# First attention layer: three query tiles of heads 0 to 15 first, projections and v tiles laid out over the steps

## The chip, the cores and the metric

One core of one Trainium2 chip runs the whole program. The metric is the device time of one execution in microseconds (us). Every run also has a span (first to last instruction, about 1.8 us less than its time) and a mean granted clock of the tensor engine (PE). Kernels are compared only within the same rounds. No run is over 1.5% above the fastest of its kernel, so all count as fast; only the state of e6, a single run, is unknown.

## The reference

Four layers in a row on x of shape 2048 x 576: attention A, gated MLP B, A, B, each with a LayerNorm ahead and a residual sum. The change touches only the first A.

```python
# A: 32 heads of 18 channels, each query sees 8 keys, 2 tokens apart
qkv = (x @ wqkv)                     # 576 -> 3*576
logits = einsum(q, k[window]) * Dh**-0.5 ; attn = softmax(logits)
o = einsum(attn, v[window]) ; return o @ wo
# B: z = gelu(x @ w_in); z1, z2 halves; z2 = layernorm(z2)
#    g = w_sp @ z2 + b_sp ; return (z1 * g) @ w_out
```

## The kernel before

Attention runs in 38 steps of manual order: a step is one tile of 112 queries and one half of the heads. Each step does logits (L_mm), the exponential on ScalarE (EXP) and the product with v (PV). All else of the layer is hung on the steps by a table: q and k projections (PG), v tiles (VW), output projection (WO), LayerNorm of the next layer (LN_...). The second half of the tokens is still being projected while the first steps run.

```python
# evacuation of a projection into staging, then moves into the row layout
if cb == 0 and d >= 3 and lent:
    stg_tiles[key] = lent[d - 3]              # first half, d=3,4: space of win2a
else:
    stg_tiles[key] = stgs[stg_rr[0] % NSTG]   # 3 staging buffers in turn
    stg_rr[0] += 1
...
for dst, src in moves:                        # up to 8 moves of 72 KB a group
    dma_rr[0] += 1
    self.dma(dst, src, eng=queues[dma_rr[0] % len(queues)])   # SP, GpSimd in turn
...
o_t = o_bufs[t % len(o_bufs)]                 # 3 buffers; VectorE writes o here
...
nc.sync.dma_start_transpose(out=oT[:, :, c0:c0 + nq], in_=o_t[:nq, :])
...
# projections of the second half: six ahead of step 0, one a step after it
pre, pgs = pgs[:6], pgs[6:]
for k_, (d, qk, cc) in enumerate(pgs):
    at(1 + k_ if li == 0 else (k_ * PG_END) // len(pgs), PG, d, qk, cc, True)
...
for s in range(NST):                          # natural order of the steps
    if s + 1 < NST:
        L_mm(s + 1)
        EXP(s + 1)
    PV(s)
    for f, a in table.pop(s, []):
        f(*a)
...
# next layer, B, tile 6 of its first pass: on GpSimd's queue
self.dma(bsp, self.B_b_sp.partition_broadcast(P), eng=nc.gpsimd)
```

bsp lies in the same buffer (ln_xn) as the last normalized tiles of layer A, so this load must wait until they have been transposed out; in the profile of before it waits 5.42 us for that.

The softmax here doesn't subtract the row's maximum and nothing guards it: scores larger than these inputs give would overflow.

## Time and profile before

| | before |
|---|---|
| time, median of 3 runs | 1190.21 us (1190.11 to 1192.29) |
| span of the profiled execution, granted clock | 1190.8 us, 0.998 |
| its time | 1192.6 us, one of its slower executions |

The lines that carry the argument stand in the prediction. First, the stretch from 60 to 70 us by the windows view: length, busy us of each engine, and as the last three figures the granted clock, the mean share of the 16 DMA engines and GB/s. Then all that VectorE waited for from 55 to 90 us (total, times, longest):

```profile
60.00:70.00 10.00, 10.00 (x177) 5.80 (x175) 6.97 (x16) 8.01 (x10) 4.50 (x8) 1.00 0.85 160
...
DVE stg L371 <- PE pp L402: 3.4, 9, 0.4
DVE rec L463 <- PE O_ps L457: 2.3, 7, 0.4
```

The reader is to see PE full, the DMA engines at 0.85, and a VectorE that waits only for PE, never for a transfer.

### The profile page before, as it was taken

How to read it: one execution, taken by the hardware profiler on the slowest of the kernel's cores; microseconds unless marked ns; L12 is line 12 of the kernel's file. 1: busy time of each engine (PE TensorE's matmuls, PEld its weight loads, DVE VectorE, ACT ScalarE, POOL GpSimd, SP SyncE). 2: the span in 40 equal slices, each digit the busy share in tenths (PEclk: the TensorE clock that was granted, in tenths of full speed). 3: DMA queues.
4: the chain of work that ended last, by engine and by line, in shares of the span. 5: the costliest groups of instructions: out<-in, count | busy, mean ns of one | idle time of the engine just before them, and what ended most of it. 6: DMA issues, size and time to landing. Idle time of an engine off the chain costs nothing.

```text
span 1190.8 us, 20761 instructions
## 1 busy us (share of the span) xinstructions
PE 1180.2 (99%) x8554; PEld 620.6 (52%) x8554; DVE 547.4 (46%) x1206; ACT 376.6 (32%) x593; POOL 281.5 (24%) x383
## 2 busy tenths in 40 slices
PE   8999999999999999999999999999999999999998
PEld 5567544444444444457755775444444444444677
DVE  8688587333233233245556786753233233233311
ACT  5578677210110110202156786760110110111000
POOL 4768685000000000001153877530000000000000
PEclk9999999999999999999999999999999999999999
DMA  8989992000000000049645999900000000000332
GB/s 195 200 163 199 181 224 65 23 4 9 12 12 12 12 1 11 12 139 291 169 98 117 203 227 196 202 14 9 12 12 1 12 12 12 12 1 28 125 105 73
DMA packets 178104, 101.21 MB, mean 85 GB/s; under 512 B 134336, under 2 KB 159360, under 8 KB 178009
## 3 DMA queue, kind: packets, MB, share of 16 engines
q1 hardware_dynamic: 165144, 78.13, 30.6%
q0 software_dynamic: 6512, 16.00, 5.4%
q10 hardware_dynamic: 6352, 5.75, 1.6%
q8 instruction: 67, 1.10, 0.4%
q14 instruction: 29, 0.23, 0.1%
HBM read 42.39 MB, written 16.53 MB: 49 GB/s over the span
## 4 chain that ended last, share of the span: by engine, by line
PE 94%; DMA 3%; POOL 1%; ACT 0%; issue 0%; SPq 0%; DVE 0%; ACTq 0%; DVEq 0%
PE pg L887 42%; PE pz L869 12%; PE po L941 12%; PE pz L791 11%; PE pp L402 5%; PE pw L494 3%; PE O_ps L457 3%; PE pv L379 3%; PE L_ps L437 2%; DMA oT<-o_t 2%; PE pzs L791 1%; DMA QK<-win2a 1%; POOL QK L77 1%; DMA wqk_sb<-in_A_wqkv_dram 1%; ACT P_sb L446 0%
## 5 line engine op out<-in xcount | busy, mean ns | idle before, releaser
L887 PE MATMUL pg<-Wq,Z 128*128 128x512 bf16 x2304 | 502.8, 379 | 0.0
L887 PEld LDWEIGHTS <-Z 128*128 128x128 bf16 x2304 | 225.3, 98 | 272.0
L891 DVE TENSOR_TENSOR g_tmp<-pg,ln_xn 128x512 f32<-128x512 f32 x144 | 99.6, 692 | 429.2 <-PE pg L887 429.2
L881 ACT ACTIVATE z1T<-pz 128x1024 bf16<-128x1024 f32 x72 | 73.7, 1024 | 513.8 <-PE pz L869 513.6
L77 POOL DMA_DIRECT2D wout<-in_B_w_out_dram x4 | 4.3, 1064 | 604.6 <-PE pg L887 604.6
L941 PE MATMUL po<-wout,Z 128*128 128x288 bf16 x1152 | 141.4, 286 | 0.0
L446 ACT ACTIVATE P_sb<-L_ps 128x896 bf16<-128x896 f32 (+1 forms) x152 | 126.7, 887 | 41.2 <-PE L_ps L437 40.6
L869 PE MATMUL pz<-xnT,w 128*128 128x512 bf16 (+1 forms) x640 | 136.0, 380 | 0.0
L941 PEld LDWEIGHTS <-Z 128*128 128x128 bf16 x1152 | 112.7, 98 | 28.8
L791 PEld LDWEIGHTS <-xnT 128*128 128x128 bf16 (+1 forms) x800 | 66.2, 97 | 81.0 <-issue 23.7
L791 PE MATMUL pz<-win2a,xnT 128*128 128x512 bf16 x384 | 104.8, 380 | 0.0
L892 DVE TENSOR_TENSOR Z<-g_tmp,z1T 128x512 bf16<-128x512 f32 x144 | 99.6, 692 | 9.7
L869 PEld LDWEIGHTS <-w 128*128 128x128 bf16 (+1 forms) x640 | 51.1, 97 | 80.0 <-issue 27.1
L402 PE MATMUL pp<-xnT,wqk_sb 128*128 128x512 bf16 x360 | 83.8, 382 | 0.5 <-DMA wqk_sb<-in_A_wqkv_dram 0.5
L805 ACT ACTIVATE zp<-pz 128x1024 bf16<-128x1024 f32 x64 | 65.5, 1024 | 36.6 <-PE pz L791 32.8
L951 DVE TENSOR_TENSOR x_new<-po,xo 128x288 f32<-128x288 f32 (+1 forms) x64 | 28.8, 455 | 87.6 <-PE po L941 83.5
L791 PE MATMUL pz<-win2b,xnT 128*128 128x512 bf16 (+1 forms) x256 | 65.7, 380 | 0.0
L807 DVE CUSTOM_DVE_ANT_0 Z<-zp 128x1536 bf16<-128x1536 bf16 x32 | 56.6, 1769 | 13.1 <-ACT zp L805 13.0
L77 POOL DMA_DIRECT2D QK<-stg x81 | 50.7, 631 | 36.3 <-DVE stg L371 21.0
L379 PE MATMUL pv<-wv_sb,xnT 128*128 128x288 bf16 (+1 forms) x380 | 55.8, 285 | 0.0
L242 POOL TENSOR_SCALAR ln_xn<-x_new,ln_mv,ln_rstd 128x576 bf16<-128x576 f32 x23 | 52.8, 2294 | 2.0
L402 PEld LDWEIGHTS <-wqk_sb 128*128 128x128 bf16 x360 | 33.2, 98 | 37.2 <-DMA wqk_sb<-in_A_wqkv_dram 1.0
(114 smaller groups left out, 916.9 us busy)
## 6 DMA issues: line engine op xcount, KB each, us to landing
xres<-x_new SPq DMA_DIRECT2D x48, 288.0 KB
xo<-xres SPq DMA_DIRECT2D x32, 288.0 KB
wout<-in_B_w_out_dram POOLq DMA_DIRECT2D x4, 1296.0 KB, 8.5
xo<-xres SPq DMA_DIRECT2D x8, 576.0 KB
w<-in_B_w_in_dram SPq DMA_DIRECT2D x16, 256.0 KB
QK<-stg POOLq DMA_DIRECT2D x53, 72.0 KB, 4.4
QK<-stg SPq DMA_DIRECT2D x41, 72.0 KB
xo<-in_A_x_dram SPq DMA_DIRECT2D x8, 288.0 KB
```

The source lines that it names most:

```text
L77: return eng.dma_start(out=out, in_=in_)
L379: nc.tensor.matmul(pv[:nk, 0:288], lhsT=self.xnT[:, c, QT * t:QT * t + nk], rhs=wv_sb[:, c, hh * 288:(hh + 1) * 288], start=(c == 0), stop ...
L402: nc.tensor.matmul(pp[:, :], lhsT=w, rhs=self.xnT[:, c, PADL + cc * 512:PADL + (cc + 1) * 512], start=(c == 0), stop=(c == 4))
L446: nc.scalar.activation(out=P_bufs[(2 * s + jp) % 4][:nk, :, :, 0:nq], in_=Lv[:nk, :, :, 0:nq], func=ACT.Exp, scale=scale)
L791: nc.tensor.matmul(pzvs[ci][:, sub * 512:sub * 512 + w], lhsT=self.xnT[r0:r1, c, PADL + i * P:PADL + (i + 1) * P], rhs=win2(c)[r0:r1, c0 + ...
L805: nc.scalar.activation(out=zp[:, c0:c0 + cn], in_=pzvs[ci][:, 0:cn], func=ACT.Gelu_apprx_tanh, accum_out=sums[:, ci:ci + 1])
L869: nc.tensor.matmul(pz1s[q // 2][:, q % 2, :], lhsT=w1[r0:r1, c, sub * P:(sub + 1) * P], rhs=self.xnT[r0:r1, c, PADL + q * 512:PADL + (q + ...
L881: nc.scalar.activation(out=z1T[:, q2 * 512:(q2 + 2) * 512], in_=pz1s[q2 // 2][:, :, :].rearrange("p a b -> p (a b)"), func=ACT.Gelu_apprx_ ...
L887: nc.tensor.matmul(pg[:, :], lhsT=Z[:, jj, i, sub * P:(sub + 1) * P], rhs=Wq[q][:, i, :], start=(i == 0), stop=(i == NS - 1))
L891: nc.vector.tensor_tensor(out=tmp[:], in0=pg[:, :], in1=bsp[:, qs], op=ALU.add)
L892: nc.vector.tensor_tensor(out=uT(jj)[:, sub, qs], in0=tmp[:], in1=z1Ts[jj, sub][:, qs], op=ALU.mult)
L941: nc.tensor.matmul(acc[hh], lhsT=uT(j // 2)[:, j % 2, i * P:(i + 1) * P], rhs=wouts[j // NJH][:, j % NJH, hh * 288:(hh + 1) * 288], start= ...
```

## The change

Its intent: let the first steps run on heads 0 to 15, whose rows are there early, and fill the steps that the exponential paces (1.85 us a step for 1.43 us of PE's work from 80.47 to 87.85 us of before) with projections, v tiles and output projections. Core of the diff:

```diff
+        seq = list(range(NST))
+        if li == 0:
+            seq[0:6] = 0, 2, 4, 1, 3, 5
...
-            self.load_wqk(nc.sync)
+            self.load_wqk(nc.sync, ("k", "q0", "q1", "k1"))
...
-            nvw0, nvw = 4, 9
+            nvw0, nvw = 4, 8
...
-        pre, pgs = pgs[:6], pgs[6:]
+        npre = 4 if li == 0 else 6
+        pre, pgs = pgs[:npre], pgs[npre:]
+        pg_at = ((0, 1, 3, 4, 5, 6, 6, 7, 7, 8, 8, 9, 10, 11, 12, 12) if li == 0 else ...)
...
-                if li == 0 and t == nvw:
-                    at(13 * hh, VW, t, hh, True)
...
+                    k_ = 2 if t == nvw else 12 + hh if t == nvw + 1 else 2 * t - 5 + hh
...
-            s = 2 * t + (6 if li == 0 and t < 10 else 5 if ...)
+            s = 10 + 2 * i if li == 0 and i < 8 else 2 * t + (5 if ...)
...
-                at(max(s + 4, 24 + (5 * i) // 4) if li == 0 else s + 4, LN_T, i)
+                at(s + 4 if li > 0 or i > 12 else 19 + 2 * i if i < 8 else 35 + (i - 8) // 2, LN_T, i)
         if li == 0:
+            for k_, part in ((2, (0, 0)), (3, (0, 1)), (5, (4, 0)), (6, (4, 1))):
+                at(k_, self.fill_window_rows, QK, 1, (part,))
...
+            at(0, lambda: nc.gpsimd.tensor_copy(out=rstds[:, 0:1], in_=self.xnT[:, 0, ...]))
+            w2l = self.load_win2a(nc.gpsimd)
```

The small GpSimd copy near the end reads the last transposed input, so that the six win2a weight loads behind it on GpSimd start only when that input has landed.

More of the change, by code (lines that the diff above doesn't have):

```diff
@@ L185, in make_ident, with fill_window_rows @@
                                 base=0, pattern=[[-1, P]], channel_multiplier=1)
-    def fill_window_rows(self, QK, half):
+    def fill_window_rows(self, QK, half, parts=((0, 0), (0, 1), (4, 0), (4, 1))):
         nc, n = self.nc, self.cfg.S // 2
@@ L193, in fill_window_rows @@
         c0 = PADL + half * n
-        for g0 in (0, 4):
-            for a in range(2):
-                nc.vector.tensor_copy(out=QK[:, a, g0:g0 + 4, c0:c0 + n].rearrange("p g (k x) -> p g k x", x=256),
-                                      in_=self.pat[:, a, None, None, PADL:PADL + 256].to_broadcast([P, 4, n // 256, 256]))
+        for g0, a in parts:
+            nc.vector.tensor_copy(out=QK[:, a, g0:g0 + 4, c0:c0 + n].rearrange("p g (k x) -> p g k x", x=256),
+                                  in_=self.pat[:, a, None, None, PADL:PADL + 256].to_broadcast([P, 4, n // 256, 256]))
     def H_tile(self, name):
@@ L284, in zero_right, with load_wqk @@
         nc.vector.memset(R["wo"][64:128, 4, :], 0.0)
-    def load_wqk(self, eng):
+    def load_wqk(self, eng, names=("k", "q", "k1")):
         R = self.right
-        for c0, n, w0 in ((D, 512, D + 64), (0, D, 0), (D + 512, 64, D)):
+        parts = dict(k=(D, 512, D + 64), q=(0, D, 0), q0=(0, 256, 0), q1=(256, D - 256, 256), k1=(D + 512, 64, D))
+        for c0, n, w0 in (parts[k_] for k_ in names):
             self.dma(R["wqk"][:, :, w0:w0 + n], self.A_wqkv[0:512, c0:c0 + n].rearrange("(c p) n -> p c n", p=P), eng=eng)
@@ L425, in layer_A @@
         NST = 2 * NT
+        seq = list(range(NST))
+        if li == 0:
+            seq[0:6] = 0, 2, 4, 1, 3, 5
+        pbi = {s: 2 * k_ for k_, s in enumerate(seq)}
         L_tiles = {}
@@ L445, in EXP @@
                 Lv = L_ps[:, :, 0:4 * QT].rearrange("p a (b c) -> p a b c", c=QT)
-                nc.scalar.activation(out=P_bufs[(2 * s + jp) % 4][:nk, :, :, 0:nq], in_=Lv[:nk, :, :, 0:nq], func=ACT.Exp,
+                nc.scalar.activation(out=P_bufs[(pbi[s] + jp) % 4][:nk, :, :, 0:nq], in_=Lv[:nk, :, :, 0:nq], func=ACT.Exp,
                                      scale=scale)
@@ L457, in PV @@
                         nc.tensor.matmul(O_ps[:, idx * (DH + 1):(idx + 1) * (DH + 1)],
-                                         lhsT=P_bufs[(2 * s + jp) % 4][:nk, jj, ftl, :],
+                                         lhsT=P_bufs[(pbi[s] + jp) % 4][:nk, jj, ftl, :],
                                          rhs=v_ext[:nk, t, 16 * hf + idx, :], start=True, stop=True)
@@ L509, in LN_XN @@
                 k_, m = divmod(i - 4, 3)
-                xn = stgs[(2 + k_) % NSTG][:].rearrange("p a b -> p (a b)")[:, 640 * m:640 * (m + 1)]
+                xn = stgs[(1 + k_) % NSTG][:].rearrange("p a b -> p (a b)")[:, 640 * m:640 * (m + 1)]
             tails[i]["xn"] = self.ln_xn(tails[i]["x"], P, mv, rstd, nmr, eng="pool", xn=xn)
@@ L648, in layer_A @@
             nvw0, nvw = 0, 4
-        for t in range(nvw0, nvw - (1 if li == 0 else 0)):
+        for t in range(nvw0, nvw):
             for hh in range(2):
-                VW(t, hh, li == 0)
+                VW(t, hh, li == 0 and t > 5)
         pieces = []
@@ L667, in layer_A @@
         PG_END = 14
-        pre, pgs = pgs[:6], pgs[6:]
+        npre = 4 if li == 0 else 6
+        pre, pgs = pgs[:npre], pgs[npre:]
+        pg_at = ((0, 1, 3, 4, 5, 6, 6, 7, 7, 8, 8, 9, 10, 11, 12, 12) if li == 0
+                 else [(k_ * PG_END) // len(pgs) for k_ in range(len(pgs))])
         for k_, (d, qk, cc) in enumerate(pgs):
-            at(1 + k_ if li == 0 else (k_ * PG_END) // len(pgs), PG, d, qk, cc, True)
+            at(pg_at[k_], PG, d, qk, cc, True)
         for t in range(nvw, NT):
             for hh in range(2):
-                if li == 0 and t == nvw:
-                    at(13 * hh, VW, t, hh, True)
-                else:
-                    at(2 * t - 2 + hh, VW, t, hh, 2 * t - 2 + hh >= PG_END and hh == 0)
+                if li == 0:
+                    k_ = 2 if t == nvw else 12 + hh if t == nvw + 1 else 2 * t - 5 + hh
+                else:
+                    k_ = 2 * t - 2 + hh
+                at(k_, VW, t, hh, k_ >= PG_END and hh == 0)
         for i in range(NS):
             t = -(-(i + 1) * P // QT) - 1
-            s = 2 * t + (6 if li == 0 and t < 10 else 5 if t < NT - 5 else 4 if t < NT - 3 else 3)
+            s = 10 + 2 * i if li == 0 and i < 8 else 2 * t + (5 if t < NT - 5 else 4 if t < NT - 3 else 3)
             at(s - 5, XO, i)
@@ L686, in layer_A @@
             if i < NS - 1:
-                at(max(s + 4, 24 + (5 * i) // 4) if li == 0 else s + 4, LN_T, i)
+                at(s + 4 if li > 0 or i > 12 else 19 + 2 * i if i < 8 else 35 + (i - 8) // 2, LN_T, i)
         if li == 0:
+            for k_, part in ((2, (0, 0)), (3, (0, 1)), (5, (4, 0)), (6, (4, 1))):
+                at(k_, self.fill_window_rows, QK, 1, (part,))
             at(0, self.load_wo, nc.sync)
-            for f in reversed(self.load_win2a(nc.gpsimd)):
-                at(0, f)
+            at(0, lambda: nc.gpsimd.tensor_copy(out=rstds[:, 0:1], in_=self.xnT[:, 0, PADL + S - 1:PADL + S]))
+            w2l = self.load_win2a(nc.gpsimd)
+            for k_ in (3, 5, 4, 2, 1, 0):
+                at(0, w2l[k_])
         at(PG_END + 2, alloc_win2b)
@@ L698, in layer_A @@
             if k_ == (2 if li == 0 else 0):
-                L_mm(0)
-                EXP(0)
-            PG(d, qk, cc, li > 0 or k_ < 4, q2)
-            if li == 0 and k_ == 3:
-                self.fill_window_rows(QK, 1)
-        if li == 0:
-            VW(nvw - 1, 0, False)
-            VW(nvw - 1, 1, False)
+                L_mm(seq[0])
+                EXP(seq[0])
+            PG(d, qk, cc, True, q2)
         for s in range(NST):
             if s + 1 < NST:
-                L_mm(s + 1)
-                EXP(s + 1)
-            PV(s)
+                L_mm(seq[s + 1])
+                EXP(seq[s + 1])
+            PV(seq[s])
             for f, a in table.pop(s, []):
```

## The prediction

> **What bounds the kernel now.** I read the page's engine table first, then the granted clock by slice, then the matmul engine's timeline of the first attention layer, because the diff acts only where the layer index is 0 (the other attention layer gets the same lists as before).
>
> ```profile
> PE 1180.2 (99%) x8554; PEld 620.6 (52%) x8554; DVE 547.4 (46%) x1206; ACT 376.6 (32%) x593; POOL 281.5 (24%) x383
> ...
> L446 ACT ACTIVATE P_sb<-L_ps 128x896 bf16<-128x896 f32 (+1 forms) x152 | 126.7, 887 | 41.2 <-PE L_ps L437 40.6
> ```
>
> PE has work in 1180 of 1190.8 us: it is the bound, and the change gives it the same matmuls in another order (the built programs have the same number of PE instructions). So the change can win only what PE loses to waits, to stretched groups and to a slow clock. 1190.8 - 1180.2 = 10.6 us is idle in the whole program. The exponential (L446) takes 0.92 us for a full tile here, and each attention step needs two of them.
>
> The places of loss, in order of time:
>
> ```profile
> 14.47 7.73 PE L402 MATMUL pp<-xnT,wqk_sb 128*128 128x512 bf16 x35 [0.55 <-DMA wqk_sb<-in_A_wqkv_dram]
> ...
> 47.28 0.89 PE L437 MATMUL L_ps<-QK 32*128 32x112 bf16 x15
> 48.86 0.22 PE L437 MATMUL L_ps<-QK 32*128 32x112 bf16 x1 [0.69 <-DMA QK<-win2a]
> ...
> 50.90 2.29 PE L402 MATMUL pp<-xnT,wqk_sb 128*128 128x512 bf16 x5
> ...
> 82.71 0.37 PE L437 MATMUL L_ps<-QK 32*128 32x112 bf16 x8 [0.27 <-ACT P_sb L446]
> ...
> 98.69 0.37 PE L437 MATMUL L_ps<-QK 32*128 32x112 bf16 x8 [0.32 <-ACT P_sb L446]
> ...
> 125.22 0.79 PE L494 MATMUL pw<-wo_sb,oT 128*128 128x288 bf16 x5 [0.59 <-DMA oT<-o_t]
> ...
> 131.51 1.39 PE L494 MATMUL pw<-wo_sb,oT 128*128 128x288 bf16 x10 [1.23 <-DMA oT<-o_t]
> ```
>
> Columns: start, duration, what, and in brackets the idle time before it. The reader is to see a wait for the q weights; the second logits group (heads 16 to 31 of tile 0) held by its q/k rows, 16 matmuls taking from 47.28 to 49.01 where a free group takes 0.33; a projection of 2.29 us where its neighbours take 1.24; small waits for the exponential; and waits for the transposed output at the end. The windows by the microsecond explain the 2.29:
>
> ```profile
> 48.00:49.00 1.00, 0.32 (x5) 0.14 (x2) 1.00 (x2) 0.90 (x1) 1.00 (x2) 1.00 1.30 223
> ...
> 51.00:52.00 1.00, 1.00 (x5) 0.31 (x3) 0.71 (x2) 1.00 (x2) 0.05 (x1) 0.50 1.06 395
> 52.00:53.00 1.00, 1.00 (x3) 0.15 (x1) 0.00 (x0) 0.33 (x1) 0.00 (x0) 0.50 1.09 286
> ```
>
> The first figure after the length is PE, the third from the end the granted clock: half, some 2 us after PE was only a third busy. No other five-microsecond window of the program has a clock below 1.
>
> [...]the four windows from 50 to 54 have 0.76, 0.50, 0.50 and 0.54, which makes 0.5 + 1 + 1 + 0.9 = 3.4 us at half.[...]at 99.99 VectorE had waited 1.59 us for an output transpose[...]
>
> **The change part by part.** Clean costs from the chain of waits: logits group 0.33, PV group 0.49, one q/k projection 1.09, one v half tile 0.62, one output half tile 0.61.
>
> (a) q weights in two pieces. The first load shrinks from 576 to 256 columns: the 0.55 us wait should mostly go. I count 0.3, as it pulls the whole start forward only if nothing else is late.
>
> (b) Order 0, 2, 4, 1, 3, 5. The late rows belong to heads 16 to 31. Before, 6 projections, one logits group and 2 v halves stood between the v stretch and that logits group; after, 6 projections, 3 logits groups and 2 PV groups. That is 2x0.33 + 2x0.49 - 2x0.62 = +0.4 us of cover, and the last of those rows no longer share the DMA engines with the six 288 KB weight loads, which began at 45.99 and now wait for the last transposed input. The loss was 49.01 - 47.28 - 0.33 = 1.4; I expect 0.9 to 1.0 left. Gain 0.4.
>
> (c) The clock. The slow stretch cost 2.29 - 1.24 = 1.05 on the projection and about 0.25 on the groups around it, 1.3. [...]I give an even chance that it goes: gain 0.65.
>
> (d) Even spreading. From 53.13 to 65.73 six steps took 12.60, 2.10 each, where PE's work is 1.09 + 0.33 + 0.49 = 1.91: the loop logits, two exponentials (2 x 0.92 plus hand-over), logits sets the step. Loss 0.19 x 7 = 1.3. From 80.47 to 87.85 four steps without projection or v took 7.38, 1.85 each against 0.33 + 0.49 + 0.61 = 1.43: loss 1.6. From 96.45 to 102.59 three steps, two without output projection, took 6.14 against 4.93: loss 1.2, part of it the late output transpose. In all 4.1. After, I count by the table of steps: steps 0, 1, 3, 4, 5, 9 with one projection lose 0.19 each (1.1), step 14, which has no v half, 0.4, steps 33 and 34, whose v halves went earlier, 0.8; the output projections of tiles 0 to 7 now fill steps 10 to 25 without a gap. Left 2.3, gain 1.8.
>
> (e) VectorE: the pattern fill of the second half, 4 copies of 1.22 us, moves from one block into steps 2, 3, 5, 6. The fullest, step 6, has 0.72 (reciprocal and scaling) + 2 x 0.69 + 1.22 = 3.3 us for 3.0 of PE: up to some 1 us of lag, which the four single banks should absorb. No gain, a risk.
>
> (f) End of the layer: waits of 0.59 and 1.23 for output transposes stay; there is less v work beside them now. I count 0.
>
> Sum: 0.3 + 0.4 + 0.65 + 1.8 = 3.15 us. 1190.2 - 3.15 = 1187.1.
>
> **The rivals.** First: the wait only moves. If the rows of heads 16 to 31 land no earlier than 48.8 (their last issue, at 44.65, waited for an earlier transfer, and the chain of waits goes back over the queue to the evictions of about 26 us), the early start earns nothing, the clock still drops, and at the end the moved v halves lengthen the wait for transposes. Then some 1 us remains: 1189. For it: the page's chain shows these transfers as the setter. Against: there are three more groups of PE work before it. Second: VectorE or the staging buffers become the wait. Projections now come in pairs at steps 6 to 8, and the staging buffer of step 7 was sent off only at step 4; a queue-and-land time of 4.4 us (page, transfers of 72 KB) against about 7 us of steps is close once Pool's six weight loads of 0.85 us each stand ahead. [...]1 to 3 us come back: 1190 to 1191. Third: the whole loss goes, the clock stays up, no wait for the rows: 1.4 + 1.3 + 3 + 0.5 gives 6 us, 1184.
>
> **Range and chances.** The prediction is 1187.1 us; the range 1184.0 to 1190.2 spans the best and nearly the worst rival. A change of 2% is 24 us; everything that PE loses in this layer is about 11, so faster by over 2% has a chance of 0.01, slower (a hang-up of the queues I don't see) 0.01, within 2% 0.98.
>
> **What would show it.** Right: no or shorter wait at the fourth logits group (tile 0, heads 16 to 31), no half clock near 50 us, no exponential waits between 80 and 101, and the first matmul of the next layer, now at 129.67, some 3 us earlier, with everything after it unchanged in length. Wrong: a bracket with a transfer of staging rows before a VectorE eviction, PE waits for evictions in steps 6 to 8, waits for output transposes above 2 us at the end, or a second slow-clock stretch. The number fails most easily in (c), all or nothing, and in (d), where the loop may pace steps that I take as full.

The length of the half-clock stretch: by windows of 0.25 us the clock is 1.00 up to 50.50, 0.50 to 0.53 from there to 53.75 and 0.64 in the window after. VectorE's wait of 1.59 us ahead of 99.99: that PE was late by it was not shown. The even chance in (c) is the author's estimate, and the trace shows for it only that half clock began some 2 us after a microsecond with PE at 0.32. The sum came to 0.3 + 0.4 + 0.65 + 1.8 = 3.15 us, and so to 1187.1 us.

Three more readings have their figures here. In (b), the weight loads were issued from 45.99 us on, the last row move landed at 48.8 us, and the DMA share from 48 to 49 us was 1.30; that parting them would help was an estimate. In (d), that the exponentials set the step rests on the step times quoted there and on PE's three waits for them from 53 to 103 us, 0.9 us in all. In (e), the four single banks are four tiles of the kernel (`bufs=4`), and that they absorb the lag was an estimate.

## The result, and the profile after

| | before | changed |
|---|---|---|
| median in the first rounds | 1190.28 us (1190.11 to 1192.29, 4 runs) | 1192.87 us (1191.88 to 1194.37, 4 runs) |
| span, clock of the profiled execution | 1190.8 us, 0.998 | 1190.2 us, 0.999 |
| ratio of fast runs, 95% interval | | 1.0019 (1.0002 to 1.0036) |

Ratios are the mean time of one kernel's fast runs over that of the other's fast runs of the same rounds, so not quite the ratio of the medians quoted. Within 2% the two are the same, as predicted; but the time is 5.8 us above the predicted 1187.1 and outside the range. That the two profiled spans are nearly equal is chance: the execution profiled of before was one of its slow ones.

PE's timeline of the changed kernel (start, duration, group, in brackets the idle time ahead of it), at the places that answer to those shown of before:

```profile
12.94 8.80 PE L402 MATMUL pp<-xnT,wqk_sb 128*128 128x512 bf16 x40
...
47.41 0.65 PE L441 MATMUL L_ps<-QK 32*128 32x112 bf16 x16
...
73.60 0.77 PE L498 MATMUL pw<-wo_sb,oT 128*128 128x288 bf16 x5 [1.56 <-DVE stg L371]
80.98 0.37 PE L441 MATMUL L_ps<-QK 32*128 32x112 bf16 x8 [0.43 <-ACT P_sb L450]
...
151.65 0.81 PE L798 MATMUL pz<-win2a,xnT 128*128 128x512 bf16 x3 [1.59 <-ACT zp L812]
```

The wait for the q weights is gone: 40 projection matmuls in one piece. The fourth logits group (tile 0, heads 16 to 31), at 47.41, has no wait. From 80 to 101 us one wait for the exponential is left, 0.43 us, where before there were three of 0.85 us together. But two stops are new, 1.56 us behind VectorE's eviction into staging and 1.59 us in the next layer, behind the activation of a z tile (the zp stop). The same views as before, from 60 to 70 us and of VectorE's waits from 55 to 90 us, and three steps of the chain of waits ahead of the stop at 73.60:

```profile
60.00:70.00 10.00, 9.69 (x131) 5.04 (x129) 6.66 (x14) 6.46 (x8) 6.14 (x10) 1.00 1.20 169
...
DVE stg L371 <- DMA QK<-stg: 6.1, 2, 3.5
DVE x_new L501 <- PE pw L498: 2.5, 2, 2.0
...
63.88 0.79 SPq L77
...
64.72 8.02 DMA QK<-stg
...
72.86 0.70 DVE stg L371
```

VectorE now waits 6.1 us for moves out of the staging buffers; one of them, issued by the SP queue, took 8.02 us to land; and the DMA engines' share is 1.20: over 1, so the times of the packets under way add up to more than one per engine. The last figure of the line, what was moved, hardly rose, from 160 to 169 GB/s: the packets took longer, they did not carry much more.

The stop at 151.65 has its cause on GpSimd. Its lines in the changed kernel:

```profile
146.25 0.64 POOL L77 DMA_DIRECT2D ln_xn<-in_B_b_sp_dram x1 [6.60 <-DMA xnT<-ln_xn]
146.92 0.59 POOL L829 TENSOR_TENSOR z_rstd<-z_rstd,neg_half 128x1 f32<-128x1 f32 x1
```

The bias-row load waits 6.60 us for the last transposes of the LayerNorm output, and the small z_rstd operation, on which the normalization and in the end PE depend, stands behind it. In the kernel before that load started at 147.00 with 5.42 us of waiting, 11.7 us after PE's last output projection (done at 135.31); in the changed kernel it started 13.7 us after it (132.58). PE came 2.7 us earlier and the load only 0.75 us; so the load lagged 2.0 us more behind PE, and what had been hidden was now a stop. The load's line before:

```profile
147.00 0.64 POOL L77 DMA_DIRECT2D ln_xn<-in_B_b_sp_dram  x1 [5.42 <-DMA xnT<-ln_xn]
```

A table from PE's timelines, worked out: for each stretch the distances from start to start of PE's groups, less their clean cost (the clean costs of the prediction). The last row is the time from the end of the last output projection to the first matmul of the spatial product (pg), less its shortest value of 77.09. The columns are the profiled executions of before (two), of the changed kernel (three), and of the changed kernel with the projections as before (two, explained below). A recount from the traces gives the same cells within 0.5 us. Each of three columns holds a stretch of 3.4 us at half clock, which stretches PE's groups (ten output matmuls took 2.16 us in e1, 1.39 before): before near 51 us, e1 from 129 to 133 us, e2 from 74 to 78 us.

| PE time lost, us | before | before, e1 | changed | changed, e2 | changed, e13 | e11 | e14 |
|---|---|---|---|---|---|---|---|
| 40 to 55 | 2.8 | 1.7 | 1.2 | 1.6 | 1.7 | 2.9 | 2.0 |
| 55 to 78 | 1.1 | 1.1 | 2.8 | 3.9 | 4.2 | 1.4 | 2.2 |
| 78 to 103 | 3.4 | 3.1 | 2.2 | 1.7 | 2.9 | 1.9 | 1.7 |
| 103 to 138 | 2.8 | 3.4 | 1.3 | 1.7 | 2.0 | 2.3 | 1.8 |
| hand-over to the next layer | 0.0 | 0.0 | 1.8 | 1.6 | 1.2 | 1.1 | 0.5 |

The spreading did what it was meant to do after 78 us, and it was paid for twice: from 55 to 78 us and at the hand-over.

### The profile page after: what moved, and what is told of

Read it like the earlier page. It is cut to its first block, busy times and chain, and to the rows that moved or that the text cites. A ratio compares the mean times of both kernels' runs of the same rounds, so it can differ in the third digit from the quotient of the medians.

```text
span 1190.2 us, 20761 instructions
## 1 busy us (share of the span) xinstructions
PE 1177.7 (99%) x8554; PEld 619.9 (52%) x8554; DVE 546.0 (46%) x1202; ACT 377.2 (32%) x597; POOL 282.3 (24%) x384
## 4 chain that ended last, share of the span: by engine, by line
PE 94%; DMA 2%; DVE 2%; POOL 1%; issue 1%; ACT 0%; SPq 0%; POOLq 0%; DVEq 0%
PE pg L894 42%; PE pz L876 12%; PE po L948 12%; PE pz L798 10%; PE pp L402 5%; PE pv L379 4%; PE pw L498 3%; PE O_ps L461 2%; PE L_ps L441 2%; PE pzs L798 1%; DMA QK<-stg 1%; DMA oT<-o_t 1%; DMA xnT<-ln_xn 0%; POOL stg L241 0%; ACT P_sb L450 0%
## 5 line engine op out<-in xcount | busy, mean ns | idle before, releaser
L899 DVE TENSOR_TENSOR Z<-g_tmp,z1T 128x512 bf16<-128x512 f32 x144 | 99.7, 692 | 10.1 <-DVE g_tmp L898 0.5
L876 PEld LDWEIGHTS <-w 128*128 128x128 bf16 (+1 forms) x640 | 51.1, 97 | 80.0 <-issue 27.1
```

The source lines that it names most:

```text
L876: nc.tensor.matmul(pz1s[q // 2][:, q % 2, :], lhsT=w1[r0:r1, c, sub * P:(sub + 1) * P], rhs=self.xnT[r0:r1, c, PADL + q * 512:PADL + (q + ...
L899: nc.vector.tensor_tensor(out=uT(jj)[:, sub, qs], in0=tmp[:], in1=z1Ts[jj, sub][:, qs], op=ALU.mult)
```

## The experiments

Eighteen runs were made, on four chips; six of them repeat a kernel (e1 the one before, e2 and e13 the changed one, e6, e14 and e17 earlier variants); runs that stand in one group shared their rounds. "V waits" are the waits of VectorE from 55 to 90 us for transfers.

### First group: are the result and its waits repeatable, and does the tail count?

**e1_before_again**: the kernel before, unaltered.

> The unchanged kernel once more, for a second profile and ten more times. The profile on record had one stretch of half clock (3.4 us, about 1.3 us lost) and its run took 1192.6 us where the other runs took 1190.1 to 1190.4. Theory C (chance events): the usual run has no half-clock stretch or no long wait for q/k rows, so part of the predicted gain was never in the median; then this profile, if its run takes about 1190.2, has a clock of 1.00 near 50 us and a span near 1188.5. Rival: the half clock is there in the fast runs too (span near 1190.8 or clock 0.5 near 51 us with a run near 1190.2), and the loss of the changed kernel lies elsewhere.

1192.16 us (1191.26 to 1194.92), ratio 1.0004. Half clock at 50 us, a term of the prediction, is not in its profile (nor in those of e4 and e8): it was an accident of the execution that had been profiled. The profile of e1 has such a stretch elsewhere, from 129 to 133 us. The wait for the q weights, the prediction's term (a), is not in these three profiles either.

**e2_after_again**: the changed kernel, unaltered.

> The changed kernel once more, for a second profile and to see whether its runs again fall into two groups near 1191.9 and 1194. Theory A (tail): PE stops about 1.6 us some 20 us into the next layer, waiting for the activation of a z tile whose buffer Pool has not released, in this profile too. Theory B (staging): a wait of VectorE for q/k rows to leave a staging buffer stops PE 1 to 3 us near 71 us in this profile too. If one of the two is missing here while the time is the same, it is not the cause of the loss.

1193.04 us (1191.38 to 1193.70), ratio 1.0005 (0.9987 to 1.0023). Two theories stood at this point: A, the gain is lost at the hand-over to the next layer (the zp stop); B, it is lost to the staging buffers, reused too early. The profile has both: a stop of 1.72 us at 74.10 on the eviction into staging, V waits of 5.3 us for staging and 1.2 us for oT, the DMA share from 60 to 70 us at 1.17, and a zp stop of 1.44 us.

**e3_after_bsp_sp** and **e4_before_bsp_sp**: in the changed kernel and in the one before,

```diff
-                self.dma(bsp, self.B_b_sp.partition_broadcast(P), eng=nc.gpsimd)
+                self.dma(bsp, self.B_b_sp.partition_broadcast(P), eng=nc.sync if li == 1 else nc.gpsimd)
```

> The changed kernel with one line of the next layer altered: the load of the bias row, which stands at the head of Pool's queue there and waits for the last input transposes, goes to the SP queue (first mixer layer only). Theory A: Pool releases the z tiles in time, the stop of 1.6 us goes, and the time falls by 1.0 to 1.8 us against e2. Theory B: the stop near 71 us is the whole loss and this changes the time by less than 0.4 us.

> The same line altered in the kernel before, where the profile shows no stop of PE in the next layer although Pool waits 5.4 us for the same load. Theory A: the time stays within 0.4 us of e1, since nothing there waited. If it falls by more than 1 us, the load held up the kernel before as well, and the gain of e3 says nothing of the change.

e3: 1193.26 us (1190.78 to 1197.47), ratio 1.0016; e4: 1192.69 us (1190.21 to 1196.08), ratio 1.0011. In e3 the stop on zp is gone and the hand-over is back at 77.10 us, so the cause of that stop is shown. (In this execution PE came late, at 139.3 us, which alone could hide it; e17, with the same edit and PE at 133.2 us, has 77.09 us as well.) The time did not follow: the executions spread over 6.7 us, and the one profiled had a stop of 3.68 us on staging and two stretches at half clock (mean clock 0.994). In e4 there was nothing to gain. So the tail alone does not explain the result.

### Second group: is it the staging buffers?

**e5_after_lent** and **e6_after_lent_bsp** (its label is a slip: it ran the same kernel as e5, as its expectation says): the changed kernel, with the second halves of d=3 and d=4 staged in two input buffers that are free by then.

```diff
                 if cb == 0 and d >= 3 and lent:
                     stg_tiles[key] = lent[d - 3]
+                elif cb == 1 and d >= 3 and lent:
+                    stg_tiles[key] = spent[d - 3][:]...   # spent = [x1, x3]
```

> The changed kernel with one thing taken away: the second-half q and k projections of channel groups d=3 and d=4 are staged in two spent input buffers (free since the first LayerNorm), so they no longer wait until the moves of the first half have left the staging buffers. Theory B (the compressed projections reuse staging too early): the stop of the projections on VectorE between 60 and 80 us (1.56, 1.72 and 3.68 us in the three looks at the changed kernel) is under 0.3 us, VectorE waits under 0.5 us on the moves QK<-stg there, the last projection of the first layer ends by 70 us, and the span is 1.5 us or more under the 1190.2 to 1191.3 us of the changed kernel if no chance stretch at half clock falls in. Theory A (the gain is lost only at the hand-over to the next layer): the last PV of the first layer comes 1 to 2 us earlier, but the stop on zp (1.4 to 1.6 us) grows to 2 to 3 us and the span stays within 1 us of the changed kernel.

> Second look at the same kernel as the run before it, for the waits alone: the stop on staging is again under 0.3 us if theory B holds, and the zp stop again at 1.4 us or more if theory A holds as well.

e5: 1192.89 us (1190.64 to 1196.13), ratio 1.0011 (0.9995 to 1.0027); e6, one run, 1194.60 us. The staging wait is gone and the time is not better. VectorE's waits for transfers in e5, and where PE stopped:

```profile
DVE o_t L470 <- DMA oT<-o_t: 5.0, 2, 3.3
DVE x_new L503 <- DMA xo<-in_A_x_dram: 3.6, 1, 3.6
...
61.80 0.58 PE L404 MATMUL pp<-xnT,wqk_sb 128*128 128x512 bf16 x1 [1.84 <-DVE o_t L470]
...
86.79 0.55 PE L463 MATMUL O_ps<-v_ext,P_sb 128*128 128x19 bf16 x16 [1.80 <-DVE x_new L503]
```

Two other transfers took its place, the transpose of the attention output and the load of the residual: VectorE waited 5.0 and 3.6 us for them, and PE 1.84 and 1.80 us for VectorE. Theory B, staging alone, falls. The profile of e6 differs: PE waited 1.53 us for rows at 49.42, half clock followed, and then the DMA share from 60 to 70 us was only 0.96 and VectorE's waits for transfers 2.4 us.

**e7_after_lent_bsp**: e5 with the edit of e3. **e8_before_lent**: the kernel before with the edit of e5.

> Both suspected causes taken away: spent input buffers as staging, and the bias row of the second layer loaded by the SP queue, so that GpSimd's queue is not held up by it. If both theories hold, neither the stop on staging nor the stop on zp is in the profile, the distance between the last PV and the first PE group of the second layer is back to about 77 us (before: 77.1; changed: 78.9), the span is 1187 to 1188.5 us and the time 1188 to 1190 us, 0.15 to 0.4% under the kernel before. If the time is still that of the kernel before although both stops are gone, a third cause is at work.

> Control: the kernel before with the same spent buffers. VectorE waited there only 0.8 us for staging and the tensor engine not at all, so both theories expect the same time within 0.15% (1190 to 1192 us on this chip) and the same waits.

e7: 1192.96 us (1189.48 to 1195.91), ratio 1.0014; the hand-over is at 77.09 us, but V waits are 4.1 us for oT and 2.9 us for xo, with a stop of PE of 2.24 us at 84.40. A third cause was at work, as its expectation put it. e8: 1191.03 us, ratio 0.9997: no change, as the control should have it.

### Third group: what makes the transfers land late?

Theories by now: the SP queue is full of issues (C1), the DMA engines are full (C2), the tile order shortens the reuse of the three o buffers from 5 to 3 steps (D), or the compressed projections are the root of it all.

**e9_lent_moves_1to2**: e5 with the moves of the second half 1 to 2 on SP and GpSimd.

```diff
-            at(pg_at[k_], PG, d, qk, cc, True)
+            at(pg_at[k_], PG, d, qk, cc, True, q2 if li == 0 else (nc.sync, nc.gpsimd))
```

> Changed kernel with spent buffers as staging (as e5), and the moves of the second token half shared 1 to 2 between the SP and the GpSimd queue in place of 1 to 1. In e5 and e6, where staging was free, VectorE waited 3.34 us for oT<-o_t and 3.60 us for an xo load in place of staging. Theory C1 (the SP queue, which issues the moves one after the other at about 0.8 us each, with the oT transposes and xo loads among them, is full from 51 to 84 us): with a third fewer moves on SP it has gaps again, the oT and xo waits of VectorE between 55 and 90 us fall from 5 to 9 us to under 2 us, no stop of the tensor engine over 0.5 us there, last PV of the first layer by 127.5 us, span about 1188.5 us. Theory C2 (the DMA engines themselves are full): the same bytes move, so the waits stay at 3 us or more, on whatever lands last. Theory D (the tile order shortens the reuse of the three o buffers): the 3.3 us wait for oT<-o_t near 61 us stays, the xo wait may go.

1195.15 us (1193.93 to 1196.55), ratio 1.0029. VectorE's waits for oT and xo fell to 1.5 and 1.0 us (5.0 and 3.6 in e5), so the SP queue had its part. But the moves now land late from the other queue, and PE waits for the rows itself:

```profile
91.05 0.62 PE L443 MATMUL L_ps<-QK 32*128 32x112 bf16 x2 [2.29 <-DMA QK<-x_in]
```

**e10_lent_w2late**: e5 with the win2a loads at steps 17 to 27.

```diff
-            for k_ in (3, 5, 4, 2, 1, 0):
-                at(0, w2l[k_])
+            for n_, k_ in enumerate((3, 5, 4, 2, 1, 0)):
+                at(17 + 2 * n_, w2l[k_])
```

> Changed kernel with spent buffers as staging (as e5), and the six win2a loads (1.7 MB) issued at steps 17 to 27, after the moves, in place of step 0. Theory C2 (DMA engines full from 45 to 80 us): their share in 50 to 60 us falls, the moves and transposes land sooner, the waits of VectorE for oT and xo fall under 2 us, span about 1188.5 us, unless the later loads crowd the steps after 90 us. Theories C1 and D: the SP queue is as full as in e5 and the o buffers are reused as early, so the waits of 3 us stay.

1198.62 us (1196.96 to 1203.64), ratio 1.0064. With 1.7 MB taken out, the DMA share from 50 to 60 us fell to 0.45 and from 60 to 70 us to 0.90; the oT wait near 61 us went, and V waits fell to 1.8 us. In the later steps, where the loads now ran, PE itself waited for output transposes:

```profile
108.87 1.38 PE L500 MATMUL pw<-wo_sb,oT 128*128 128x288 bf16 x5 [6.54 <-DMA oT<-o_t]
118.33 1.38 PE L500 MATMUL pw<-wo_sb,oT 128*128 128x288 bf16 x5 [3.42 <-DMA oT<-o_t]
```

So the moves land sooner with the loads out of this stretch: the median landing of GpSimd's 72 KB moves from 55 to 80 us was 4.1 us, against 8.4 us in e5. That it is the capacity of the DMA engines that they fight for is the author's reading and was not shown by itself. That the moved loads themselves cause the later stops is argued, not shown: the share there, 1.15 from 100 to 110 us, is no higher than the 1.29 of e13 (the changed kernel), where nothing stopped. How much of the lateness is the engines and how much the SP queue is not separated by e9 and e10; each helped.

**e11_after_proj_as_before**: the changed kernel with the projections of the second half as before, on its own staging buffers. With them the pattern fills, four VectorE copies of 1.2 us, move from steps 2, 3, 5, 6 to 0, 1, 3, 4; what that does alone was not tried, and one such copy stands in the chain of waits ahead of the stop at 73.60, so it is an open rival.

```diff
-        npre = 4 if li == 0 else 6
+        npre = 6
-        pg_at = ((0, 1, 3, 4, 5, 6, 6, 7, 7, 8, 8, 9, 10, 11, 12, 12) if li == 0
+        pg_at = (tuple(range(1, 13)) if li == 0
-            for k_, part in ((2, (0, 0)), (3, (0, 1)), (5, (4, 0)), (6, (4, 1))):
+            for k_, part in ((0, (0, 0)), (1, (0, 1)), (3, (4, 0)), (4, (4, 1))):
```

> Changed kernel with one part undone: the q and k projections of the second token half stand as in the kernel before (six ahead of step 0, then one a step at steps 1 to 12), with its own staging buffers, no spent ones; tile order, split q weights, spread v tiles and the bias row as changed. If the compression of the projections (two a step at steps 6 to 8) is the root, under B, C1 and C2 alike, the waits on staging, oT and xo between 55 and 90 us are gone (under 1 us each), and the span is 1188.5 to 1189.5 us even with the zp stop. If theory D (o buffers, tile order) holds, the wait for oT<-o_t near 61 us stays at 2 us or more.

1191.16 us (1190.14 to 1191.72), ratio 0.9993 (0.9981 to 1.0005). Staging waits 0.3 us in all, xo none; oT 1.4 us, which did not stop PE. DMA share from 60 to 70 us: 0.96.

**e12_lent_natural_order**: e5 with `seq[0:6] = 0, 2, 4, 1, 3, 5` taken out.

> Changed kernel with spent buffers as staging (as e5), and the tile order of the first six steps undone (0,1,2,3,4,5). Theory D: between a query tile's transpose and the next use of its o buffer lie 5 steps again in place of 3, so VectorE's wait for oT<-o_t near 61 us (3.34 us in e5, 2.49 us in e7) goes, and the xo wait with it; the row wait at step 1 comes back (0.4 to 1.4 us). Theories C1 and C2: the waits of VectorE for oT or xo of 2 to 3 us stay between 55 and 90 us.

1196.49 us (1194.98 to 1196.82), ratio 1.0037. The oT wait near 61 us is gone, as theory D has it, but it is gone in e10 and 0.2 us in e6 as well, both with the tile order; so D alone does not make it. An xo wait of 2.13 us stays, and the rows of heads 16 to 31 are missing:

```profile
45.16 0.22 PE L443 MATMUL L_ps<-QK 32*128 32x112 bf16 x1 [1.57 <-DMA QK<-win2a]
47.32 0.74 PE L443 MATMUL L_ps<-QK 32*128 32x112 bf16 x9 [1.95 <-DMA QK<-win2a]
```

With two projections fewer ahead of step 0 the natural order would wait 3.5 us for rows. The tile order hides that.

### Fourth group: the root, beside the changed kernel

**e13_after_third**: the changed kernel. **e14_proj_as_before_again**: e11. **e15_proj_as_before_bsp_sp**: e11 with the edit of e3. **e16_proj_as_before_natural_order**: e11 with the natural order of the steps.

> The changed kernel unaltered, beside its own variants in the same rounds. If the compressed projections are the root, its profile shows again a stop of 1.5 us or more on the tensor engine between 60 and 90 us and the zp stop of about 1.5 us, VectorE waits over 4 us for moves there, and its time is 1192.5 to 1193.5 us, 1 to 2 us above the two kernels with the projections of before. If the 1.9 us between it and e11 was only chip or chance, the three agree within 0.7 us.

> Repeat of e11 (projections of the second token half as before, all else as changed), beside the changed kernel. Root in the compression: again no stop over 1 us between 55 and 120 us, no run over 1193 us, 1190.5 to 1191.5 us, ratio to before 0.999 to 0.9998. Chance: within 0.7 us of the changed kernel.

> e11 with the tail's cause taken away too: the bias row of the second layer is loaded by the SP queue. Both theories together: the zp stop (0.94 us in e11, 1.59 and 1.44 us in the changed kernel) is gone, nothing over 1 us is left, span 1188 to 1189 us, time 1189.5 to 1190.3 us, some 0.15% under the kernel before and some 0.25% under the changed one. If the load on the SP queue costs as much elsewhere, it is level with e14.

> e11 with the tile order undone as well (0,1,2,3,4,5): what the order is worth by itself. The prediction's term: a row wait at step 1 of 1.0 to 1.4 us comes back, +0.4 us or a little more. If early rows are as late as in e12 (1.57 and 1.95 us), +2 to +3 us. The wait of VectorE for oT<-o_t near 61 us (1.45 us in e11) is gone.

| same rounds | median (range), us | ratio to before (95%) | DMA share 60 to 70 us | hand-over, us |
|---|---|---|---|---|
| before | 1191.57 (1189.84 to 1194.40) | | | |
| e13, changed | 1192.47 (1191.67 to 1195.51) | 1.0012 (0.9998 to 1.0026) | 1.23 | 78.34 |
| e14, projections as before | 1190.85 (1189.18 to 1193.98) | 0.9996 (0.9980 to 1.0011) | 0.94 | 77.63 |
| e15, and bias row on SP | 1190.49 (1189.05 to 1192.73) | 0.9986 (0.9974 to 0.9999) | 0.88 | 77.10 |
| e16, as e14, natural order | 1192.43 (1190.50 to 1193.71) | 1.0003 (0.9990 to 1.0017) | 0.98 | 77.56 |

The window from 60 to 70 us and VectorE's longest waits for transfers, of e13 and then of e14:

```profile
60.00:70.00 10.00, 7.55 (x106) 3.88 (x105) 7.50 (x15) 4.86 (x7) 5.50 (x8) 1.00 1.23 185
...
DVE o_t L468 <- DMA oT<-o_t: 3.8, 1, 3.8
DVE x_new L501 <- DMA xo<-in_A_x_dram: 2.7, 1, 2.7
```

```profile
60.00:70.00 10.00, 9.89 (x172) 5.48 (x172) 6.76 (x16) 7.76 (x10) 2.98 (x6) 1.00 0.94 158
...
DVE o_t L468 <- DMA oT<-o_t: 1.8, 1, 1.8
```

In e13 the changed kernel, with no edit, waits for oT and xo, where in its two earlier profiles it waited for staging: which transfer is the last changes from execution to execution, that they are late does not. The transpose that stopped PE in e13 was issued at 51.55 us, while the six win2a loads were being issued (48.8 to 53.8), and took 10.1 us to land; in e14 the first transpose is issued at 56.7 us, after them. By the time alone the compression is not proven: e13 is 1.9 us above e14 by the means of six runs each, with ranges that overlap. Over all rounds the changed kernel has ratios of 1.0019, 1.0005 and 1.0012, the projections as before 0.9993 and 0.9996. The order of the steps is worth 1.6 us by the medians of e14 and e16, 0.9 us by the means of their six runs each and 0.8 us by their profiled spans (1187.9 and 1188.7); this too is within the spread of the runs. e14 missed one thing expected, that no run is over 1193 us (two were); the profile of e15 missed its expected span of 1188 to 1189 us (1191.0), with 6.8 us at half clock from 48.6 us on.

### Fifth group: the reverse, and the best version once more

**e17_proj_as_before_bsp_again**: e15. **e18_before_proj_compressed**: the kernel before with the compressed projections alone.

```diff
-        pre, pgs = pgs[:6], pgs[6:]
+        npre = 4 if li == 0 else 6
+        pre, pgs = pgs[:npre], pgs[npre:]
+        pg_at = (0, 1, 3, 4, 5, 6, 6, 7, 7, 8, 8, 9, 10, 11, 12, 12)
-            at(1 + k_ if li == 0 else ...
+            at(pg_at[k_] if li == 0 else ...
```

> Repeat of e15, the fastest version so far, beside another kernel in the same rounds: both causes taken away, so no stop over 1 us between 55 and 160 us, no stop on zp, 1189.5 to 1191 us, ratio to before 0.998 to 0.9995. If e15 was chance, it is level with before.

> The reverse of e11 and e14: the kernel before with one part of the change alone, the compressed projections (four ahead of step 0, the rest at steps 0,1,3,4,5,6,6,7,7,8,8,9,10,11). Root in the compression: the DMA share between 60 and 70 us rises from 0.85 to 0.98 (before and its variants) to 1.1 to 1.25 (changed: 1.20, 1.17, 1.23), VectorE waits 4 us or more for moves, oT or xo between 55 and 90 us, and the time is 1 to 2.5 us over before, 1192.5 to 1194 us. If it needs the other parts of the change too (tile order, v tiles): within 0.7 us of before, share under 1.0.

e17: 1191.03 us (1189.69 to 1192.17) against 1192.33 us of before in the same rounds, ratio 0.9990 (0.9978 to 1.0002). With e15 that makes 0.9986 and 0.9990: both times under the kernel before, by 1.1 and 1.3 us of the medians, the interval of the second just reaching past 1. It is the fastest version found, though not clearly faster than e14.

e18: 1197.82 us (1193.89 to 1199.31), ratio 1.0041 (1.0025 to 1.0058). Slower, but neither expectation fits. The DMA share from 60 to 70 us was 0.66, and VectorE did not wait for transfers there. PE waited for rows instead, and half clock followed, and again near 133 us:

```profile
46.99 0.49 PE L437 MATMUL L_ps<-QK 32*128 32x112 bf16 x8 [1.56 <-DMA QK<-win2a]
```

So the compression costs in either kernel, but not in one way. Alone, it starts the steps before the rows of heads 16 to 31 are there. Together with the tile order, which hides that, the steps run on into the crowded stretch. There it meets the win2a loads, which the change holds back until 49 to 51 us (they were issued from 50.7 to 55.0 us in the changed kernel's first profile, from 48.8 to 53.8 us in e13, from 46.0 to 51.1 us in before). A share of 1.15 to 1.23 from 60 to 70 us was seen with all three together (changed, e2, e3, e5, e7, e13; e9 had 1.02, and e6, held up before it, 0.96); with the loads moved away (e10), the natural order (e12, 0.52), or the projections as before (e11, e14 to e17), it was under 1. The share alone is no proof: the kernel before reaches 1.20 as well, from 100 to 110 us, and e14 has 1.10 from 50 to 60 us, where no stop of PE followed. The landing of the 72 KB moves on GpSimd's queue from 55 to 80 us parts the runs more clearly: medians of 6.1 to 8.9 us with all three together (but 4.7 in e6), 4.2 to 4.9 us in the kernel before, e1, e4 and e8, 3.8 to 4.7 us with one of the three undone (e10 to e12, e14 to e17) or with the compression alone (e18). That holding back the loads is a part of it is thus supported by e10 but was not tried by itself in the changed kernel, and stays open.

## Why the prediction was wrong

**Base, and term (c).** The term assumed that half clock near 50 us was a standing loss with an even chance to go. It was in one execution and not in the profiles of e1, e4 and e8; three of four profiles had nothing to gain there. This part of the sum, 0.65 us, was read off one profile, and no second one was asked for.

**(a)** the same slip. The wait for the q weights that it was to remove, 0.55 us, is in the first profile of before and in e18 (0.58), but not in e1, e4 and e8. The first logits start at 40.5 to 40.7 us in the three profiles of the changed kernel, and at 40.5 to 41.3 in five of before and its variants. The means, 40.6 and 41.0, differ by 0.4 us against 0.3 counted, but that is within the scatter of the five.

**(b)** right in direction in the changed kernel: no row wait or a short one (0.39 us in e2, 0.27 in e13), but e6, with the same order, has one of 1.53 us. By itself it measures 0.8 to 1.6 us (e14 against e16), not clear of noise, against the 0.4 counted; in the changed kernel it is spent on the two projections that no longer stand ahead of step 0.

**(d)** right in direction, and its size was met by luck. From 78 to 103 us, where it counted losses of 1.6 and 1.2 us and left 0.4, the table gives a gain of 1.0 us (mean of the two profiles of before less that of the three of the changed kernel, 3.25 - 2.27). From 103 to 138 us, where it foresaw a loss of 0.8 us, the table gives a gain of 1.4 us (3.1 - 1.7). That belongs to (f), which said that the waits for output transposes stay: they were 0.59 and 1.23 us before and are in none of the three profiles of the changed kernel. It is also less certain than it looks: e1 has its half clock there, and the recount, taken without e1 and with e4 and e8 (1.8 and 2.6 us lost), leaves 0.5 us.

**(e), with the second rival**, is the main step that failed: "up to some 1 us of lag, which the four single banks should absorb. No gain, a risk." The prediction named the mechanism, staging sent off at step 4 and wanted at step 7, and priced it with the median landing of 4.4 us as the page has it for the kernel before. The landing time is not a constant of the transfer: between 55 and 80 us the median of GpSimd's 72 KB moves was 4.5 us before and 6.7 us in the changed kernel, and one move on SP took 8.02 us. The lines of the two (the last figure is the median from issue to landing):

```profile
QK<-stg POOLq DMA_DIRECT2D x13, 72.0 KB, 4.5
...
QK<-stg POOLq DMA_DIRECT2D x13, 72.0 KB, 6.7
```

In e2 and e13 that median was 7.5 and 6.1 us, in e1, e4 and e8 4.2 to 4.9. Cost: 2.5 us from 55 to 78 us (1.1 lost before, 3.6 in the mean of three). And other buffers did not help: with them (e5) the wait went to the next transfers, 5.0 us for oT and 3.6 us for xo.

**(f), and "everything after it unchanged in length"**, failed as well. The time from the last output projection to the first pg grew from 77.1 to 78.3 to 78.9 us, because the bias-row load on GpSimd's queue, hidden before, now started 13.2 to 13.7 us after PE's last output projection, against 11.7 before, 10.7 in e1 and 12.2 in e8. In every profile with the load on that queue the hand-over exceeds 77.1 us by just what this distance has over 11.9 us. It is not that PE came earlier: in e1 PE was done at 133.98 us and nothing was lost, in e2 at 133.79 us and 1.6 us were. What grew is the way to the last LayerNorm transposes, for which the load waits 6.6 to 7.2 us in place of 4.4 to 5.7. The change moves these transposes too (LN_T in the diff); whether that is the reason was not tried. Cost: 1.2 to 1.8 us; e3, e7, e15 and e17 bring it back to 77.1.

Sum of the profiles: start 0.4 + 0.75 (40 to 55) + 1.0 + 1.4 - 2.5 - 1.5 = -0.45 us, a small loss where 3.15 us of gain had been predicted. As a check, the first pg starts at 212.4 and 211.1 us in the two profiles of before (e4: 209.9, e8: 210.7) and at 211.4, 212.5 and 212.0 us in the three of the changed kernel, 0.9 us later in the mean. The timed medians put the loss at 0.9 to 2.6 us, with noise of that same size, and the version with both causes undone (e15, e17) gains 1.1 to 1.3 us by its medians.

## What to carry to other kernels

Moving projections closer together can bring their transfers into the way of others: as many 72 KB moves were issued from 55 to 80 us as before (25), and those on GpSimd's queue landed 2.2 us later (medians of 6.7 and 4.5 us). So before spreading PE's work, list what else is under way in the stretch that the work goes to, and price a landing by what it may be there, not by the median of the kernel before. When a removed wait comes back at another transfer, stop giving buffers and look at what else is being moved at that time (e10: the moves landed in 4.1 us in place of 8.4, though e10 as a whole took 1198.62 us). When the order of work ahead of a hand-over changes, follow every chain that arrives there and not only the bounding engine's, such as transposes for which a load waits (6.60 us here) that stands ahead of a small operation on GpSimd. And read a term off one profile only after a second one shows it.

## The half clock in these traces

What sets off a stretch at half clock is not shown here; the length of the idle time ahead of it does not decide by itself. In e2 a full stop of 1.72 us was followed by half clock; in e17 PE was busy 0.51, 0.56 and 0.45 of three microseconds from 46 us on, and 3.4 us at half clock followed; in e13 a stop of 2.25 us left the clock at 1.00. The stretches measured were 3.4 us long (before, e1, e2, e17) or about twice that (e15, from 48.6 to 55.5 us). Windows of 1 us (the second figure is the length, the third PE's busy time, the third from the end the clock), e13 first, then e17:

```profile
60.00:61.00 1.00, 0.05 (x3) 0.00 (x0) 0.00 (x0) 1.00 (x2) 0.00 (x0) 1.00 1.65 239
61.00:62.00 1.00, 0.00 (x0) 0.00 (x0) 0.21 (x1) 0.36 (x1) 0.00 (x0) 1.00 0.80 155
62.00:63.00 1.00, 0.65 (x3) 0.35 (x5) 1.00 (x3) 0.00 (x0) 0.00 (x0) 1.00 1.02 182
```

```profile
46.00:47.00 1.00, 0.51 (x20) 0.48 (x17) 0.90 (x4) 1.00 (x2) 0.00 (x0) 1.00 1.18 206
47.00:48.00 1.00, 0.56 (x18) 0.33 (x12) 1.00 (x2) 1.00 (x2) 0.00 (x0) 1.00 1.25 214
48.00:49.00 1.00, 0.45 (x16) 0.35 (x14) 0.68 (x3) 1.00 (x2) 0.00 (x0) 1.00 0.59 104
49.00:50.00 1.00, 0.84 (x3) 0.44 (x5) 0.24 (x1) 0.15 (x1) 0.88 (x3) 0.81 0.75 157
50.00:51.00 1.00, 1.00 (x11) 0.16 (x13) 0.00 (x0) 0.00 (x0) 0.97 (x2) 0.50 1.07 387
```
